# Placing VectorE operations that share GpSimd's port as they become due, and moving the last head-pair products into the last score banks

## Chip, cores and metric

One core of one Trainium2 chip. The metric is the device time of one execution in microseconds; lower is better. "Span" is the time from the first to the last instruction in a profiled execution, about 2 us less than the time.

## The reference

Two independent attention layers read different inputs, and their outputs stand side by side. S = 2048, D = 512, 32 heads of 16.

```python
# A: multi-query attention, one key/value head for 32 query heads
q = (x @ wq) -> heads;  k = x @ wk;  v = x @ wv
p = softmax(q k^T * 16**-0.5);  a = concat_heads(p v) @ wo
# B: linear attention with a learned feature map
phi = concat(softmax(u @ w_phi), softmax(-(u @ w_phi)))   # for u = q and u = k
b = concat_heads((phi_q @ (phi_k^T v)) / (phi_q @ sum(phi_k) + 1e-6)) @ wo
return concatenate([a, b], axis=-1)                        # [1, 2048, 1024]
```

Part A has 32 x 2048 x 2048 scores to exponentiate: 2048 tiles of 128 x 512. That is most of the time.

## The kernel before

The kernel contains a scheduler that runs when the program is built. It keeps a list of jobs with estimated durations, an estimated clock `te` per engine, and places one job after the other; the order that it finds is then fixed in the program. The chip never sees the estimates, only the order and the semaphore waits.

Jobs that matter here: `qk` (scores, PE), `ex` (exponentials of two tiles, ACT), `dq`/`dz`/`dS`/`dpv` (four tiles, a "quad", exponentiated by VectorE with a bit trick, shifted three times by GpSimd, then accumulated), `ac` (copy of a finished accumulation out of PSUM), `rc` and DMAs (its denominators inverted and broadcast), `on` (multiply by them), `qw` (three steps of divisions of part B), `kvfin`.

```python
LOCK = ("dS", "qw", "on", "kvfin")      # VectorE jobs that use the port shared with GpSimd
...
# run(): when can job j start on its engine?
t = max(r, self.pe_from(j, te) if eng == "pe" else te)     # r: ready, te: engine free
j.asked = t
if eng == "pool" or j.name[0] in self.LOCK:
    t = max(t, self.te_port)                               # and the port free
...
s, j = min(picks, key=lambda p: (p[0], p[1].asked))
if j.eng == "dve" and j.name[0] in self.LOCK:              # a GpSimd job about due? take that
    s, j = next((p for p in picks if p[1].eng == "pool" and p[1].asked <= s + self.NEAR
                 and self.te_port <= s + self.NEAR), (s, j))
...
# an accumulation leaves PSUM only after the multiply two blocks earlier: f_accS has two buffers
self.job(("ac", sc), "dve", 0.60, lambda: self.finish_sc(sc), prio=0,
         after=[("on", sc - 2)] if sc >= 2 else [], frees=[("acc", sc)])
...
def finish_sc3(self, sc):               # "on": both inputs in SBUF
    self.add("dve", lambda v: v.tensor_tensor(out=o, in0=accS[:, r, :], in1=R[:, r, :], op=ALU.mult), ...)
    if r: self.dmas(...)                # odd blocks: f_Ot into the other rows of f_On
...
def out_part(self, i):                  # last 512 queries: three head pairs of two row blocks, early
    for A in range(3): pe.matmul(ps[:, bank, :], lhsT=On[:, A, ...], rhs=self.wo_pad[:, A, :], ...)
def finish_last(self):
    for i in (0, 2, 1, 3): ...          # the other products, then the last block's denominators
```

## Time and profile before

| | before |
|---|---|
| time, median | 712.1 us |
| exponential instructions on ACT (two tiles each) | 710 |
| quads on VectorE | 157 |
| first exponential starts / last one ends | 8.8 / 697.2 us |
| from the last exponential to the end of the span | 12.7 us |

Read it as a sum: ACT works without a break between the two times in the fourth row, so what counts is how many exponentials it gets, what gaps it has, and how long the ends are. The lines are in the prediction.

### The profile page before, as it was taken

What the parts mean: (1) busy time and instruction counts of PE and PEld (TensorE: products, weight loads), DVE (VectorE), ACT (ScalarE), POOL (GpSimd) and SP (SyncE); (2) the same over time, 40 slices, a digit from 0 to 9 for tenths busy, and PEclk for the clock granted to TensorE, in tenths of its full rate; (3) what the DMA queues carried; (4) which work ended last, traced back from release to release, by engine and by line L of the source; (5) the groups of instructions that cost most, each with busy time, mean ns of one, the idle gap of its engine ahead of it and who ended that gap; (6) DMA issues with size and microseconds to landing.
All of it is one profiled execution on the core that took longest, in us unless ns stands there. A gap on an engine that the chain in (4) does not pass through costs nothing.

```text
span 709.9 us, 20307 instructions
## 1 busy us (share of the span) xinstructions
PE 682.6 (96%) x8606; PEld 207.0 (29%) x8609; DVE 602.6 (85%) x1009; ACT 689.3 (97%) x782; POOL 498.4 (70%) x507
## 2 busy tenths in 40 slices
PE   8999999999999999998999999999999999999986
PEld 3322222222222222222233223332323233323222
DVE  4797899999899898988879978798879888998772
ACT  5999999999999999999999999999999999999994
POOL 5378777777777877575858856778685856678781
PEclk9999999999999999999999999999999999999999
DMA  6712133110111201111101221101121012112012
GB/s 125 147 11 38 32 43 75 15 10 3 8 14 13 39 2 14 11 10 13 13 5 15 35 27 17 17 7 20 10 20 21 16 13 40 24 18 29 13 10 44
DMA packets 47898, 18.42 MB, mean 26 GB/s; under 512 B 38708, under 2 KB 45940, under 8 KB 47800
## 3 DMA queue, kind: packets, MB, share of 16 engines
q1 hardware_dynamic: 45544, 16.36, 18.1%
q8 instruction: 69, 1.13, 0.7%
q10 hardware_dynamic: 2256, 0.69, 0.4%
q14 instruction: 29, 0.24, 0.1%
HBM read 2.28 MB, written 4.19 MB: 9 GB/s over the span
## 4 chain that ended last, share of the span: by engine, by line
ACT 60%; PE 31%; DVE 4%; POOL 1%; DMA 1%; SPq 1%; issue 1%; POOLq 0%; DVEq 0%
ACT f_PT L1701 57%; PE f_ps L1646 11%; PE f_ps L1866 8%; PE f_ps L1748 4%; DVE f_Z L1806 2%; ACT f_Ek L2127 2%; PE f_ps L1955 1%; PE f_ps L2319 1%; POOL f_Z L1836 1%; PE f_ps L2225 1%; ACT f_ET L2231 1%; PE f_ps L1443 1%; PE f_ps L2275 1%; PE f_ps L2300 1%; PE f_ps L1628 1%
## 5 line engine op out<-in xcount | busy, mean ns | idle before, releaser
L1701 ACT ACTIVATE f_PT<-f_ps 128x1024 bf16<-128x1024 f32 x710 | 661.9, 1124 | 4.3 <-PE f_ps L1748 2.3
L1836 POOL INT64_ADD f_Z<-f_Z x471 | 489.0, 1038 | 192.3 <-DVE f_Z L1806 153.3
L1806 DVE TENSOR_SCALAR f_Z<-f_ps 128x512 int16<-128x512 f32 x628 | 418.2, 684 | 74.3 <-PE f_ps L1646 69.9
L1646 PE MATMUL f_ps<-f_QA,f_KR 32*128 32x512 bf16 x2048 | 284.9, 385 | 13.0 <-ACT f_PT L1701 9.4
L1866 PE MATMUL f_ps<-f_Z,f_VK 128*32 128x512 f16 x2512 | 216.8, 385 | 5.0 <-PE f_ps L1866 1.8
L1646 PEld LDWEIGHTS f_ps<-f_QA,f_KR 32*128 32x128 bf16 x2048 | 72.1, 91 | 272.4 <-ACT f_PT L1701 252.7
L1748 PE MATMUL f_ps<-f_PT,f_VA 128*32 128x512 bf16 x1420 | 133.0, 385 | 0.1
L1866 PEld LDWEIGHTS f_ps<-f_Z,f_VK 128*32 128x32 bf16 x2512 | 53.1, 94 | 95.2 <-issue 58.5
L1748 PEld LDWEIGHTS f_ps<-f_PT,f_VA 128*32 128x32 bf16 x1420 | 34.1, 94 | 50.6 <-issue 45.2
L1443 PE MATMUL f_ps<-f_ones,f_zero 128*128 128x512 bf16 (+6 forms) x109 | 21.7, 371 | 1.5 <-POOL f_zero L1462 1.3
L2286 DVE TENSOR_TENSOR f_Wk<-f_ps,f_wq 128x512 bf16<-128x512 f32 x32 | 21.7, 681 | 0.4 <-PE f_ps L2275 0.4
L2172 DVE TENSOR_TENSOR f_vS<-f_ps,f_rs 128x1024 bf16<-128x1024 f32 x16 | 21.2, 1322 | 0.0
L1449 DVE COPY f_accS<-f_ps 128x512 f32<-128x512 f32 x31 | 21.0, 677 | 0.0
L2162 PE MATMUL f_ps<-f_Bwv,f_BxT 128*32 128x512 bf16 x256 | 19.6, 383 | 0.3
L2225 PE MATMUL f_ps<-f_BxT,f_Wq 128*32 128x512 bf16 x256 | 19.6, 383 | 0.2
L1628 PE MATMUL f_ps<-f_AxT,f_wq 128*32 128x512 bf16 (+1 forms) x272 | 19.5, 371 | 0.3
L2319 PE MATMUL f_ps<-f_Bwo,f_oT 128*32 128x512 bf16 x256 | 19.6, 382 | 0.1
L2119 PE MATMUL f_ps<-f_Wk,f_BxT 128*32 128x512 bf16 x256 | 19.6, 383 | 0.0
L2231 ACT ACTIVATE f_ET<-f_ps 128x512 bf16<-128x512 f32 x32 | 19.6, 740 | 0.0
L2127 ACT ACTIVATE f_Ek<-f_ps 128x512 bf16<-128x512 f32 x32 | 19.4, 726 | 0.0
L2133 DVE TENSOR_REDUCE f_ssum<-f_Ek 128x64 f32<-128x1024 bf16 x16 | 19.3, 1206 | 0.0
L1933 DVE TENSOR_TENSOR f_On<-f_accS,f_denS 128x512 bf16<-128x512 f32 x16 | 11.2, 702 | 7.4 <-DMA f_denS<-f_denS 7.4
(96 smaller groups left out, 274.5 us busy)
## 6 DMA issues: line engine op xcount, KB each, us to landing
f_denS<-f_denS SPq DMA_DIRECT2D x124, 30.0 KB, 3.1
out_dram<-f_outB SPq DMA_DIRECT2D x16, 128.0 KB, 2.4
f_denC<-f_accS SPq DMA_DIRECT2D x124, 2.0 KB, 1.7
f_denS<-f_denC SPq DMA_DIRECT2D x124, 2.0 KB, 1.7
out_dram<-f_outA SPq DMA_DIRECT2D x15, 128.0 KB, 2.3
f_On<-f_Ot SPq DMA_DIRECT2D x60, 16.0 KB, 1.8
f_Bwv<-in_B_wqkv_dram SPq DMA_DIRECT2D x1, 512.0 KB, 4.7
f_Bwo<-in_B_wo_dram SPq DMA_DIRECT2D x1, 512.0 KB, 4.6
```

Source lines behind the costliest of these rows:

```text
L1443: mm = pe.matmul(ps[m * i:m * i + m, bank, 0:n].rearrange("p (a n) -> p a n", n=128), lhsT=zero[0:r, 0:m], rhs=rhs, start=start, stop=star ...
L1628: mm = pe.matmul(ps[32 * g:32 * g + 32, bank, a:a + n], lhsT=self.wq[:, dc, A * 128 + 32 * g:A * 128 + 32 * g + 32], rhs=xT[:, dc, qc * 51 ...
L1646: return pe.matmul(self.ps[:, bank, :], lhsT=self.KR[32 * g:32 * g + 32, sc % 2, kap * 128:(kap + 1) * 128], rhs=self.QA[32 * g:32 * g + 3 ...
L1701: self.add("act", lambda a: a.activation(out=PT[:, sl[0]:sl[0] + size, :], in_=ps[:, b0:b0 + size, :], func=ACT.Exp), reads=[("PS", b0 + i ...
L1748: mm = pe.matmul(ps[32 * g:32 * g + 32, bank, :], lhsT=VA[:, kap, :], rhs=PT[:, slots[g], :], start=start, stop=stop, tile_position=(0, 32 ...
L1806: self.add("dve", lambda v: v.tensor_scalar(out=o, in0=ps[:, bank, :], scalar1=self.Z1, scalar2=self.Z0, op0=ALU.mult, op1=ALU.add), reads ...
L1836: fn = lambda g: g.int64_add(out=b, in0=a, in1=256 * t * 0x1000100010001)
L1866: mm = pe.matmul(ps[32 * g:32 * g + 32, bank, :], lhsT=self.VK[:, t, kap, :], rhs=Zf[:, sl[g], :], start=start, stop=stop, tile_position=( ...
L2127: self.add("act", (lambda a, sg: (lambda e: e.activation(out=Ek[:, r, a, :, :], in_=ps[:, bank, :].rearrange("p (h f) -> p h f", h=32), fu ...
L2225: mm = pe.matmul(ps[32 * g:32 * g + 32, bank, :], lhsT=w[:, dc, G * 128 + 32 * g:G * 128 + 32 * g + 32], rhs=xT[:, dc, m * 512:(m + 1) * 5 ...
L2231: self.add("act", lambda e: e.activation(out=self.ET[:, sl, :], in_=self.ps[:, bank, :], func=ACT.Exp, scale=1.0 - 2.0 * a), reads=[("PS", ...
L2319: mm = pe.matmul(ps[32 * g:32 * g + 32, bank, :], lhsT=oT[:, r, C, 32 * g:32 * g + 32], rhs=self.Bwo[:, C, :], start=(C == 0), stop=(C == ...
```

## The change

The intent: a LOCK job that has waited long is no longer passed over for GpSimd work again and again; the spread of part B's work over time (`T_B`) is chosen anew for it; and at the end fewer products wait for the second-last block.

```diff
+    PATIENT = 6.0
-    T_B = (43.0, 620.0)
+    T_B = (40.0, 595.0)
@@ run()
-                        if eng == "pool" or j.name[0] in self.LOCK:
+                        if eng == "pool" or (j.name[0] in self.LOCK and t - r < self.PATIENT):
                             t = max(t, self.te_port)
...
-            if j.eng == "dve" and j.name[0] in self.LOCK:
+            if j.eng == "dve" and j.name[0] in self.LOCK and j.asked == s and s < self.te_port:
+                s = self.te_port
+            elif j.eng == "dve" and j.name[0] in self.LOCK:
                 s, j = next(...)
@@ jobs_a(), out_part(): two head pairs instead of three, after "on" 24..27 instead of 24..29
-            for A in range(3):
+            for A in range(2):
@@ new job "fa": three early terms of row blocks 0 and 2, in score banks 0 and 2, once the last scores are read
+            job(("fa", i), "pe", 0.65, ... self.out_first(2 * i) ..., after=[("on", 24 + a) for a in range(6)],
+                ok=lambda: self.last_qk is not None and ("ex", self.last_qk) in self.issued)
@@ finish_last()
-        for i in (0, 2, 1, 3):
-            terms = [(self.On[:, a, :], a) for a in range(3)] if i % 2 == 0 else []
+        for i in (1, 3, 0, 2):
+            terms = [(self.On[:, 2, :], 2)] if i % 2 else []
```

More of the change, by code (lines that the diff above doesn't have):

```diff
@@ L1241, in __init__ @@
         self.free = [4, 5, 6, 7]
-        self.part_no = None
+        self.part_no = self.last_qk = None
         self.rec = None
@@ L1555, in jobs_a @@
         for i in range(2):
-            job(("pp", i), "pe", 0.65, (lambda i: (lambda: self.out_part(i)))(i), mode="full", nb=1, prio=3.0,
-                after=[("on", 24 + a) for a in range(6)] + [("bk", 15), ("bv", 15)] + [("bq", 3, G) for G in range(4)])
+            job(("pp", i), "pe", 0.43, (lambda i: (lambda: self.out_part(i)))(i), mode="full", nb=1, prio=3.0,
+                after=[("on", 24 + a) for a in range(4)] + [("bk", 15), ("bv", 15)] + [("bq", 3, G) for G in range(4)])
             job(("ppc", i), "dve", 0.60, (lambda i: (lambda: self.out_part2(i)))(i), after=[("pp", i)], frees=[("pp", i)], prio=1)
+            job(("fa", i), "pe", 0.65, (lambda i: (lambda: self.out_first(2 * i)))(i), mode="full", prio=3.0, after=[("on", 24 + a) for a in range(6)],
+                ok=lambda: self.last_qk is not None and ("ex", self.last_qk) in self.issued)
         for sc in range(31):
@@ L1670, in next_qk @@
         if not us:
+            if self.last_qk is None:
+                self.last_qk = i - 1
             return
@@ L1973, in fn @@
             mm = None
-            for A in range(3):
-                mm = pe.matmul(ps[:, bank, :], lhsT=On[:, A, i * 256 + 128:i * 256 + 256], rhs=self.wo_pad[:, A, :], start=(A == 0), stop=(A == 2))
+            for A in range(2):
+                mm = pe.matmul(ps[:, bank, :], lhsT=On[:, A, i * 256 + 128:i * 256 + 256], rhs=self.wo_pad[:, A, :], start=(A == 0), stop=(A == 1))
             return mm
-        self.add("pe", fn, reads=[("On", A) for A in range(3)] + ["wo_pad", "wo_pad0"], writes=[("PS", bank)])
+        self.add("pe", fn, reads=[("On", A) for A in range(2)] + ["wo_pad", "wo_pad0"], writes=[("PS", bank)])
     def out_part2(self, i):
@@ L1981, in out_part2, with product, fn, out_first @@
         self.copy(self.part[:, i, :], self.ps[:, bank, :], [("PS", bank)], [("part", i)] + [("BxT", c) for c in range(4)])
+    def product(self, i, terms, start, stop):
+        ps = self.ps
+        def fn(pe):
+            mm = None
+            for n, (o, a) in enumerate(terms):
+                mm = pe.matmul(ps[:, i, :], lhsT=o[:, i * 128:i * 128 + 128], rhs=self.wo_pad[:, a, :], start=start and n == 0, stop=stop)
+            return mm
+        return fn
+    def out_first(self, i):
+        self.add("pe", self.product(i, [(self.On[:, a, :], a) for a in range(3)], True, False), reads=[("On", a) for a in range(3)] + ["wo_pad", "wo_pad0"], writes=[("PS", i)])
     def finish_last(self):
-        ps, lnd, part, oa, ACC = self.ps, self.lnd, self.part, self.outA, self.bank(("acc", 31))
+        ps, lnd, part, oa, ACC, product = self.ps, self.lnd, self.part, self.outA, self.bank(("acc", 31)), self.product
         H = 256
-        def product(i, terms, start, stop):
-            def fn(pe):
-                mm = None
-                for n, (o, a) in enumerate(terms):
-                    mm = pe.matmul(ps[:, i, :], lhsT=o[:, i * 128:i * 128 + 128], rhs=self.wo_pad[:, a, :], start=start and n == 0, stop=stop)
-                return mm
-            return fn
-        for i in (0, 2, 1, 3):
-            terms = [(self.On[:, a, :], a) for a in range(3)] if i % 2 == 0 else []
-            self.add("pe", product(i, terms + [(self.On[:, 3, :], 4)], True, False), reads=[("On", a) for a in range(4)] + ["wo_pad", "wo_pad0"], writes=[("PS", i)])
+        for i in (1, 3, 0, 2):
+            terms = [(self.On[:, 2, :], 2)] if i % 2 else []
+            kw = dict(writes=[("PS", i)]) if i % 2 else dict(accum=[("PS", i)])
+            self.add("pe", product(i, terms + [(self.On[:, 3, :], 4)], i % 2 == 1, False), reads=[("On", a) for a in range(2, 4)] + ["wo_pad", "wo_pad0"], **kw)
         for h in range(2):
```

## The prediction

> **What bounds the kernel now.** The first view is the page: busy times, then the costliest groups.
>
> ```profile
> PE 682.6 (96%) x8606; PEld 207.0 (29%) x8609; DVE 602.6 (85%) x1009; ACT 689.3 (97%) x782; POOL 498.4 (70%) x507
> L1701 ACT ACTIVATE f_PT<-f_ps 128x1024 bf16<-128x1024 f32 x710 | 661.9, 1124 | 4.3 <-PE f_ps L1748 2.3
> L1836 POOL INT64_ADD f_Z<-f_Z x471 | 489.0, 1038 | 192.3 <-DVE f_Z L1806 153.3
> L1806 DVE TENSOR_SCALAR f_Z<-f_ps 128x512 int16<-128x512 f32 x628 | 418.2, 684 | 74.3 <-PE f_ps L1646 69.9
> ```
>
> ACT computes softmax exponentials, two score tiles at a time (L1701). The table of windows (20 us each) shows ACT busy 20.00 of 20.00 in nearly all of them between 40 and 600 us, and its idle time before L1701 is 4.3 us in all. So ACT sets the pace: 661.9 / 710 = 0.932 us for two tiles. The time can shrink only if ACT gets fewer tiles, or if the few us before its first exponential (8.8 us) and after its last (697.2 us) shrink. There are 2048 tiles. VectorE does 628 of them with a bit trick (L1806) in groups of four ("quads", 157), and GpSimd makes three shifted copies of each quad (471 = 3 x 157). **The exchange rate:** one more quad on VectorE takes four tiles, or 2 x 0.932 = 1.86 us, from ACT, and costs VectorE 4 x 418.2/628 = 2.66 us. VectorE is 85% busy and idles 69.9 us waiting for scores to work on: there is room, and the question is why it is not used.
>
> The second view is the timeline of VectorE, GpSimd and the SyncE queue around 600 us. Each of the 32 accumulations ("blocks": one half of the head pairs and 512 queries) ends in a copy to f_accS, DMAs that invert and broadcast the denominator (L1892, L1903, L1909), and a multiply, L1933, called "on" in the plan.
>
> ```profile
> 593.34 3.35 SPq L1909 DMA_DIRECT2D f_denS<-f_denS  x4
> 607.07 3.39 SPq L1909 DMA_DIRECT2D f_denS<-f_denS  x4
> 621.07 1.04 POOL L1836 INT64_ADD f_Z<-f_Z  x1
> 621.62 1.03 DVE L1933 TENSOR_TENSOR f_Ot<-f_accS,f_denS 128x512 bf16<-128x512 f32 x1
> 622.57 0.68 DVE L1933 TENSOR_TENSOR f_On<-f_accS,f_denS 128x512 bf16<-128x512 f32 x1
> 623.17 0.68 DVE L1449 COPY f_accS<-f_ps 128x512 f32<-128x512 f32 x1
> ```
>
> The broadcast of block 25 was issued by 596.7 us and landed about 2.3 us later (3.1 us median from issue to landing, less its own 0.82 us of issue), so its multiply was due near 599; it ran at 621.62, and that of block 26, due near 613, right behind it. f_accS has two buffers, so block 27's copy (623.17) had to follow, and until then block 27's PSUM bank, one of four that the plan shares out, stayed held. I paired all 31 broadcasts with their multiplies: from the end of the last issue to the multiply 19.9 us on average (2.7 to 40.3), and in 13 of 29 blocks the f_accS copy came within 2 us of the multiply that it had to wait for. This is the plan's doing, not the chip's: operations in LOCK ("dS", "qw", "on", "kvfin") may only be placed where the plan's GpSimd is free, and a GpSimd job that is about due is preferred again and again.
>
> What a held bank costs shows in a table of windows: for twelve of those 13 copies, VectorE's busy time in the 10 us before the copy (first line) and in the 10 us after it (second).
>
> ```profile
> sum 120.00, DVE 100.23; mean DVE 8.35
> sum 120.00, DVE 110.03; mean DVE 9.17
> ```
>
> The third view is the end: the timeline of the SyncE queue and of VectorE, with the chain of waits, which runs through exactly these lines.
>
> ```profile
> 690.10 0.68 DVE L1933 TENSOR_TENSOR f_Ot<-f_accS,f_denS 128x512 bf16<-128x512 f32 x1
> 692.06 3.40 SPq L1909 DMA_DIRECT2D f_denS<-f_denS  x4
> 695.50 2.45 SPq L1939 DMA_DIRECT2D f_On<-f_Ot  x4
> 698.15 0.69 DVE L1933 TENSOR_TENSOR f_On<-f_accS,f_denS 128x512 bf16<-128x512 f32 x1 [7.37 <-DMA f_denS<-f_denS]
> 700.55 1.24 PE L1975 MATMUL f_ps<-f_wo_pad,f_On 128*128 128x512 bf16 x5 [0.56 <-DMA f_On<-f_Ot]
> 701.18 1.49 DVE L1449 COPY f_BxT<-f_ps 128x512 f32<-128x512 f32 x2 [2.34 <-PE f_ps L1975]
> 702.72 0.45 DVE L1999 STREAM_SHUFFLE f_ET<-f_ps 128x256 f32<-128x256 f32 x1
> ```
>
> The shuffle needs only the last accumulation, closed at 697.67 us. It starts at 702.72 because VectorE runs in order and stands behind two copies (L1449), which wait for products (L1975), which wait for the DMA of L1939.
>
> **What the Trainium skill says.** "SBUF — State Buffer", section "Who interferes with whom": a VectorE instruction with two SBUF inputs contends with a GpSimd instruction that reads SBUF, and the later one blocks until the other is done. The trace agrees: the GpSimd add above ends at 622.11, and the multiply that began at 621.62 ends 0.54 us after that and takes 1.03 us instead of 0.68. The longest multiply, 1.31 us, has the same cause. "VectorE: DVE Perf Modes", section "Why PSUM operands drop a tier": a PSUM operand rules out the two-port mode, so L1806 should not contend; its 628 instructions take 624 to 825 ns with GpSimd 70% busy. "Perfetto Trace Analysis", section "Identifying the Most-Contended Engine": matmul busy time is a poor measure. This trace bears it out in that the 96% of PE includes 21.7 us of filler on zeros (L1443), though most of PE's other work is real.
>
> **The change, part by part.**
>
> (a) Placement. A LOCK operation that was ready for 6 us (PATIENT) now competes at the time it became possible; if chosen, it starts when the plan's port is free. It removes the long starvation and leaves 6 us plus at most about one GpSimd add of 1.04 us. No instruction is added. The gain is VectorE time: raising those 13 stretches to the level after them gives 13 x (9.17 - 8.35) = 10.7 us. Part B's divisions ("qw") also finish sooner: the three steps took 20.8 us (447.3 to 468.2) and 16.1 us (591.7 to 607.8) in two of four blocks, 3.5 us in the others. 10.7 us would be 10.7 / 2.66 = 4 quads. Against it stands blocking on the port: some 25 multiplies and a few divisions are placed without regard to it; with GpSimd busy 70% and half an add of 1.04 us left on average, 35 x 0.7 x 0.52 = 13 us of VectorE at worst. I take half of that as falling into time in which VectorE waits for scores anyway, so 6.5 us or 2.4 quads lost. Net: 1.6 quads.
>
> (b) T_B. Part B's work is spread over 40 to 595 us instead of 43 to 620 (its last output copy was at 666.7). By itself this only moves VectorE load forward. But it is a retuned pair of numbers, chosen for this plan: I allow 1 quad for it, a guess. (a) and (b) together: 2.6 quads, 2.6 x 1.86 = 4.8 us, and ACT's total falls by the same.
>
> (c) The end. The early products take two head pairs instead of three (4 matmuls instead of 6), so they and their copies no longer wait for the DMA of L1939 and can run before the end. Products in banks 0 and 2 are split into three early terms (out_first) and one late. The matmuls number 20 before and after. The shuffle can start after the last multiply of L1933, 698.15 + 0.69 = 698.84 us, and what it feeds is done by 701.4 (the same steps took 702.72 to 705.28). PE then sets the end: if L1939 lands at the same 700.25, twelve products follow at 0.2125 us (sixteen took 700.55 to 703.95), to 703.1, four last ones to 703.95, and the last VectorE addition ends near 705.0 instead of 706.67: 1.7 us gained. If block 29's multiply comes early enough for L1939 to go ahead of the broadcast (L1909), the multiply at 698.84 limits: six products, the factors at 701.4, four last products, the addition to 703.0: 3.7 us gained. I take 2.4.
>
> Sum: 712.1 - 4.8 - 2.4 = 704.9.
>
> **The rivals.** (1) The port takes it back: starvation turns into blocked multiplies, each 1.0 to 1.3 us instead of 0.68, and the number of exponentials stays 710. For it: three multiplies show just this block. Against it: VectorE has 69.9 us of idle time to hide it in. Then only the end is won: 709.7. (2) Banks were the real limit: the multiplies on time free a bank for longer than the stretches I counted, VectorE reaches the 93 to 94% of its best windows (100 to 180 us: 18.2 to 19.6 of 20) everywhere. In the window of 660 us (20 to 680) it is at 579.5, 88%; solving 0.93 x (658 - 1.86 q) = 579.5 + 2.66 q gives 7.3 quads and about 696. Against it: the 10 us after a copy reach only 9.17 because delayed work is piled up there. (3) Another PE wait: out_first stands in PE's order and waits for L1939; if the plan lets it in before the last accumulation is finished, accumulation stalls behind a DMA; worth up to 3 us, so the end gains nothing: 707.
>
> **Range and chances.** The number of exponentials is decided by a greedy plan that answers chaotically to small changes: I give it 0 to 5 quads, 0 to 9.3 us, and the end 1 to 4 us. That spans 699 to 711; with rivals 2 and 3 at the edges I take 698 to 710. Faster by over 2% needs under 697.9, thus six quads and a good end: 0.11. Slower by over 2% needs some seven quads lost: 0.01.
>
> **What would show it.** L1701 some 5 fewer than 710 (x704 to x706), L1806 some 10 more than 628 (x640 or so), L1836 in step. The multiplies at most about 10 us after their broadcast, with more durations over 0.9 us than the three before. The f_accS copies evenly spaced near 21 us. The copies L1449 into f_BxT before the last exponential, the shuffle right behind the last multiply, and the time from the last exponential to the end near 10.3 us instead of 12.7. I am wrong if L1701 stays at 710 or grows (the placement is worth nothing), if it falls below 699 (rival 2), or if ACT has idle stretches of more than 5 us before its last exponential.

## The result

The change takes 706.12 us (705.97 to 706.59, 4 runs) against 712.06 us. The ratio is 0.9916, interval 0.9899 to 0.9933. (Ratios are the mean time of one kernel's runs over that of the other's of the same rounds, so not quite the ratio of the medians.) That is 5.9 us less: within 2%, inside the range, 1.2 us above the predicted 704.9.

The page of the kernel after, busy times and costliest groups, in the columns of those shown of before:

```profile
PE 678.6 (96%) x8614; PEld 205.4 (29%) x8614; DVE 609.7 (87%) x1017; ACT 686.6 (97%) x778; POOL 513.9 (73%) x513
...
L1705 ACT ACTIVATE f_PT<-f_ps 128x1024 bf16<-128x1024 f32 x706 | 658.1, 1107 | 4.4 <-PE f_ps L1648 3.3
L1840 POOL INT64_ADD f_Z<-f_Z x477 | 504.5, 1058 | 174.7 <-DVE f_Z L1810 135.4
L1810 DVE TENSOR_SCALAR f_Z<-f_ps 128x512 int16<-128x512 f32 x636 | 420.4, 682 | 55.9 <-PE f_ps L1648 51.6
```

(Lines have moved: L1701, L1806, L1836 and L1933 of before are L1705, L1810, L1840 and L1937.) VectorE took two more quads (636 tiles, 159 quads), so ACT runs 706 exponentials. VectorE waits 51.6 us for scores instead of 69.9. GpSimd's adds have become longer: 1058 ns on average instead of 1038.

The starvation is gone. From the end of a broadcast's issue to the multiply it takes 10.2 us on average instead of 19.9, at most 16.0 instead of 40.3. Before, 13 of 29 f_accS copies came within 2 us of the multiply that they had to wait for; now none does, and the copies are 16.5 to 25.8 us apart (10.2 to 33.5 before).

The end, in the timeline of the kernel after (start, duration, engine, line, output from input, count, and in brackets the idle time before it with what ended it):

```profile
688.69 3.43 SPq L1913 DMA_DIRECT2D f_denS<-f_denS  x4
...
692.16 2.45 SPq L1943 DMA_DIRECT2D f_On<-f_Ot  x4
...
694.81 0.69 DVE L1937 TENSOR_TENSOR f_On<-f_accS,f_denS 128x512 bf16<-128x512 f32 x1 [6.76 <-DMA f_denS<-f_denS]
...
695.61 0.44 DVE L2010 STREAM_SHUFFLE f_ET<-f_ps 128x256 f32<-128x256 f32 x1
...
696.87 2.77 PE L1994 MATMUL f_ps<-f_wo_pad,f_On 128*128 128x512 bf16 x12 [1.32 <-DMA f_On<-f_Ot]
...
699.47 1.03 PE L1994 MATMUL f_ps<-f_wo_pad,f_Ot 128*128 128x512 bf16 x4
```

The shuffle follows the last multiply at once. PE sets the end: its twelve products wait for the DMA of L1943, which still stands behind the broadcast (L1913).

**The sum.** I took the start and duration of every ACT instruction from the traces. An exponential follows the one before it after 0.917 us (median); "gaps" below is what the exponentials after the first took beyond 0.92 us each, summed.

| part of the span | before | after | difference |
|---|---|---|---|
| until the first exponential | 8.8 | 9.1 | +0.3 |
| exponentials x 0.92 us | 710 | 706 | -3.7 |
| gaps | 3.8 | 5.0 | +1.3 |
| other work of ACT between them (the rest) | 31.4 | 31.5 | 0.0 |
| after the last exponential | 12.7 | 9.4 | -3.3 |
| span | 709.9 | 704.5 | -5.4 |

(The row of exponentials gives counts, and the difference in us; rows are rounded.) Two thirds of what the quads were worth arrived, 2.4 of 3.7 us, and the end gave more (3.3 us). The questions for the experiments: which part did it, are the held banks really the cause, what made the new gaps, and why only two quads.

### The profile page after: what moved, and what is told of

It reads as the page before. It is cut to its first block, busy times and chain, and to the rows that moved or that the text cites. A ratio compares the mean times of both kernels' runs of the same rounds, so it can differ in the third digit from the quotient of the medians.

```text
span 704.5 us, 20334 instructions
## 1 busy us (share of the span) xinstructions
PE 678.6 (96%) x8614; PEld 205.4 (29%) x8614; DVE 609.7 (87%) x1017; ACT 686.6 (97%) x778; POOL 513.9 (73%) x513
## 4 chain that ended last, share of the span: by engine, by line
ACT 45%; PE 43%; DVE 8%; DMA 1%; SPq 1%; issue 1%; POOL 0%; DVEq 0%; POOLq 0%
ACT f_PT L1705 43%; PE f_ps L1648 15%; PE f_ps L1870 12%; PE f_ps L1752 6%; DVE f_Z L1810 4%; PE f_ps L1959 1%; PE f_ps L2330 1%; PE f_ps L2173 1%; PE f_ps L2130 1%; ACT f_ET L2242 1%; PE f_ps L1630 1%; PE f_ps L2236 1%; ACT f_Ek L2138 1%; PE f_ps L1443 1%; DVE f_vS L2183 1%
## 5 line engine op out<-in xcount | busy, mean ns | idle before, releaser
L1705 ACT ACTIVATE f_PT<-f_ps 128x1024 bf16<-128x1024 f32 x706 | 658.1, 1107 | 4.4 <-PE f_ps L1648 3.3
L1840 POOL INT64_ADD f_Z<-f_Z x477 | 504.5, 1058 | 174.7 <-DVE f_Z L1810 135.4
L1810 DVE TENSOR_SCALAR f_Z<-f_ps 128x512 int16<-128x512 f32 x636 | 420.4, 682 | 55.9 <-PE f_ps L1648 51.6
L1870 PE MATMUL f_ps<-f_Z,f_VK 128*32 128x512 f16 x2544 | 224.0, 386 | 5.7 <-PE f_ps L1870 3.1
L1870 PEld LDWEIGHTS f_ps<-f_Z,f_VK 128*32 128x32 bf16 x2544 | 54.1, 94 | 101.8 <-issue 69.1
L2297 DVE TENSOR_TENSOR f_Wk<-f_ps,f_wq 128x512 bf16<-128x512 f32 x32 | 21.7, 683 | 1.7 <-PE f_ps L2286 1.4
L1937 DVE TENSOR_TENSOR f_On<-f_accS,f_denS 128x512 bf16<-128x512 f32 x16 | 13.0, 813 | 6.8 <-DMA f_denS<-f_denS 6.8
L1443 PE MATMUL f_ps<-f_ones,f_zero 128*32 128x256 bf16 (+4 forms) x90 | 16.1, 367 | 1.3 <-POOL f_zero L1462 1.3
```

The lines of the kernel that those rows point to most:

```text
L1705: self.add("act", lambda a: a.activation(out=PT[:, sl[0]:sl[0] + size, :], in_=ps[:, b0:b0 + size, :], func=ACT.Exp), reads=[("PS", b0 + i ...
L1810: self.add("dve", lambda v: v.tensor_scalar(out=o, in0=ps[:, bank, :], scalar1=self.Z1, scalar2=self.Z0, op0=ALU.mult, op1=ALU.add), reads ...
L1840: fn = lambda g: g.int64_add(out=b, in0=a, in1=256 * t * 0x1000100010001)
L1870: mm = pe.matmul(ps[32 * g:32 * g + 32, bank, :], lhsT=self.VK[:, t, kap, :], rhs=Zf[:, sl[g], :], start=start, stop=stop, tile_position=( ...
```

## The experiments

All in one table; "tail" is from the last exponential to the end of the span, and times are medians with the ratio to the kernel before.

| run | what it is | exponentials | gaps | last exp. ends | tail | time | ratio [interval] |
|---|---|---|---|---|---|---|---|
| before | | 710 | 3.8 | 697.2 | 12.7 | 712.1 | |
| after | (a) + (b) + (c) | 706 | 5.0 | 695.1 | 9.4 | 706.1 | 0.9916 [0.9899, 0.9933] |
| end_only | (c) | 710 | 3.2 | 696.7 | 10.8 | 709.2 | 0.9955 [0.9938, 0.9972] |
| place_only | (a) | 706 | 4.9 | 695.1 | 10.4 | 706.7 | 0.9914 [0.9898, 0.9931] |
| place_end | (a) + (c) | 706 | 3.6 | 693.6 | 10.8 | 705.9 | 0.9904 [0.9888, 0.9921] |
| end_tb | (b) + (c) | 714 | 11.9 | 708.8 | 13.6 | 724.4 | 1.0173 [1.0156, 1.0190] |
| place_mul | (a), multiplies alone | 708 | 6.0 | 698.3 | 10.7 | 710.4 | 0.9969 [0.9953, 0.9986] |
| place_div | (a), divisions alone | 710 | 3.1 | 696.3 | 24.0 | 722.3 | 1.0149 [1.0132, 1.0166] |
| ring3 | before, third buffer | 704 | 7.8 | 695.9 | 30.7 | 728.0 | 1.0223 [1.0205, 1.0240] |
| no_lock | after, LOCK emptied | 702 | 11.7 | 697.8 | 9.2 | 708.9 | 0.9970 [0.9931, 1.0009] |
| no_port | after, multiplies off the port | 706 | 3.1 | 692.9 | 9.3 | 704.1 | 0.9886 [0.9870, 0.9903] |
| mul_on_gpsimd | after, multiplies on GpSimd | 702 | 367 | 1053.5 | 14.0 | 1072.1 | 1.506 [1.503, 1.509] |
| patient4 | after, patience 4, old T_B | 704 | 4.1 | 692.2 | 9.9 | 703.8 | 0.9880 [0.9863, 0.9896] |
| patient4b | patient4, T_B to 615 | 704 | 8.3 | 696.5 | 9.9 | 707.5 | 0.9932 [0.9918, 0.9945] |

### Which part: end_only, place_only, place_end, end_tb

**end_only**: the change with `PATIENT = 1e9` and the old `T_B`.

> Only part (c), the new end; placement and T_B as before. The built program has 710 exponentials, as before. My theory (the end is worth what PE and the last DMA leave, part of it): the last exponential ends as before near 697.2 us, and the time from there to the end falls from 12.7 to about 10.5 us, so 709.5 to 710.5 us in all. Rival 'the end is the whole gain': 706 to 707 us. Rival 'the early terms block PE': last exponential later than 698 us, time 711 or more.

709.16 us, 0.3 us below the expected range. The same 710 exponentials, a tail shorter by 1.9 us, and gaps shorter by 0.6 us.

**place_only**: the kernel before with the two conditions in run() and `PATIENT = 6.0` alone.

> Only part (a): PATIENT of 6 us in the plan of before; T_B and the end as before. The built program has 706 exponentials instead of 710. My theory (held banks cost quads, each worth 1.86 us): no f_accS copy waits for its multiply any more, waits of multiplies near 10 us, time 707.5 to 709.5 (2 quads, 3.7 us, less about 1 us of new waits). Rival 'the port takes it back on the chip': ACT gets idle time in place of the four exponentials, 711 to 713.

706.67 us, 0.8 us better than the expected range. The placement alone brings nearly all of the whole change, including 2.3 us of the tail, which I had put down to part (c): the multiply of block 29, no longer starved, comes earlier, and so does its DMA.

**place_end**: the change with `T_B = (43.0, 620.0)`.

> Parts (a) and (c) with T_B as before: the change less its retuned numbers. 706 exponentials, as with the whole change. My theory: T_B adds nearly nothing on the chip, so 705.5 to 707.5 us. Rival 'T_B is worth a quad or the plan's own 2.8 us': 708 to 709.5.

705.85 us, so the retuned T_B adds nothing: 0.9904 without it, 0.9916 with it, intervals overlapping. Part (c) on top of (a) is not resolved either (0.9914 and 0.9904). The profiles say why. First the timelines of the SyncE queue and of VectorE in place_only, then those in place_end:

```profile
690.08 2.45 SPq L1939 DMA_DIRECT2D f_On<-f_Ot  x4
...
692.51 0.69 DVE L1933 TENSOR_TENSOR f_On<-f_accS,f_denS 128x512 bf16<-128x512 f32 x1 [4.40 <-DMA f_denS<-f_denS]
```

```profile
682.12 3.12 SPq L1943 DMA_DIRECT2D f_On<-f_Ot  x4
...
689.67 4.00 SPq L1913 DMA_DIRECT2D f_denS<-f_denS  x4
...
695.83 0.69 DVE L1937 TENSOR_TENSOR f_On<-f_accS,f_denS 128x512 bf16<-128x512 f32 x1 [9.22 <-DMA f_denS<-f_denS]
```

In place_only the last multiply is done before the last exponential ends (695.1), and PE has what the DMA of block 29 brings at 695.2. In place_end the DMA goes ahead of the broadcast, as I had hoped for, but that puts the broadcast back, and the last multiply now comes 2.2 us after the last exponential. What one DMA gains in the queue the other loses.

**end_tb**: the change with `PATIENT = 1e9`.

> Parts (b) and (c) without (a): the new T_B and the new end with the old placement. The built program has 714 exponentials, two quads FEWER on VectorE than before. My theory: T_B was chosen for the new placement and harms the old one, 713 to 717 us. Rival 'T_B helps by itself': under 709.

724.37 us, slower still than I expected, in the direction of my theory. T_B by itself is no gain: with the old placement it costs two quads (714 exponentials) and 8.7 us of gaps against end_only.

### Which operations, and is it the held banks: place_mul, place_div, ring3

**place_mul** and **place_div**: place_only with the two new conditions for one name only.

```diff
-(j.name[0] in self.LOCK and t - r < self.PATIENT)
+(j.name[0] in self.LOCK and not (j.name[0] == "on" and t - r >= self.PATIENT))    # "qw" in place_div
-if j.eng == "dve" and j.name[0] in self.LOCK and j.asked == s and s < self.te_port:
+if j.eng == "dve" and j.name[0] == "on" and j.asked == s and s < self.te_port:    # "qw" in place_div
```

> Part (a) for the multiplies alone; divisions and kvfin stay starved; T_B and the end as before. The built program has 708 exponentials. If held banks are the main thing: about half of the quads and the earlier last DMA, 708 to 710. If the divisions are the main thing: 711 or more.

> Part (a) for the divisions alone; the multiplies stay starved; T_B and the end as before. The built program has 710 exponentials, as before. If held banks are the main thing: nothing gained, and in the plan the last multiplies come very late, so 712 to 722. If the divisions are the main thing: 709 or less.

710.39 us, just above its expected range, and 722.29 us, just above its own. The multiplies alone give one quad and the shorter tail, and lose part of that to gaps (6.0 us). The divisions alone give nothing and leave the end worse, with a tail of 24 us, because the last multiplies are starved: block 29's broadcast was issued by 678.5 us, the DMA after its multiply at 690.6, block 30's DMAs from 693.1 on, and the last multiply ran at 710.2. So the multiplies are what has to be placed. In these three orders the two together give one quad more than the multiplies alone; the rebuilt plans below show that this is not so in general.

**ring3**: the kernel before with three buffers for f_accS, f_denS and f_denC.

```diff
-    NZ = 14
+    NZ = 13
...
-after=[("on", sc - 2)] if sc >= 2 else []
+after=[("on", sc - 3)] if sc >= 3 else []
...
```

> The kernel before with a third buffer for f_accS, f_denS and f_denC, so that a late multiply holds no PSUM bank; the starvation itself stays. To make room NZ is 13 instead of 14, which gives the kernel before an identical plan. The built program has 704 exponentials. My theory (held banks are what the starvation costs): VectorE gets 3 quads more with the old placement, the last exponential ends near 692 us; but part B still ends late (starved divisions), so the end of the kernel may be longer; 705 to 711 us. Rival 'the held banks cost nothing, other things in the new placement do': last exponential at 696 us or later.

The count moved as the theory says: VectorE gets three quads more (704 exponentials). The time did not: 728.04 us. The group of exponentials on the page of ring3, then a line of its waits:

```profile
L1701 ACT ACTIVATE f_PT<-f_ps 128x1024 bf16<-128x1024 f32 x704 | 656.6, 1121 | 7.6 <-PE f_ps L1646 6.2
```

```profile
ACT f_ET L2003 <- DVE f_ET L1999: 23.8, 1, 23.8
```

After the last exponential ACT waits 23.8 us for the end's work (6.0 us before): outputs of part B are still being made after 700 us. The expected range for the time was missed for that reason, and the last exponential at 695.9 us lies between what the theory (692) and its rival (696 or later) said, so the run is evidence by its count alone. Nor is it the clean test that it was meant to be. The third buffer did not free the banks: the multiplies were put off further, to 33.6 us after their broadcast on average (66.6 at most) instead of 19.9, and 10 of 28 f_accS copies still came within 2 us of the multiply that they had to wait for, now the one three blocks earlier. Two copies right behind two multiplies, from the timeline of VectorE:

```profile
679.07 0.68 DVE L1933 TENSOR_TENSOR f_On<-f_accS,f_denS 128x512 bf16<-128x512 f32 x1
...
680.27 1.28 DVE L1449 COPY f_accS<-f_ps 128x512 f32<-128x512 f32 x2
```

One count can also be luck of one order. So the plans were built again without running them: five kernels, each over the same 32 pairs of T_B (starts 37, 40, 43 and 46; ends 560 to 630 in steps of 10). "Held" is the plan's own time from the end of a block's last accumulating product to the start of its copy, summed over 31 blocks.

| plan | quads, mean of 32 | banks held, us |
|---|---|---|
| before | 156.0 | 151 |
| third buffer (ring3) | 157.9 | 111 |
| multiplies alone (place_mul) | 158.8 | 19 |
| divisions alone (place_div) | 156.5 | 150 |
| all of LOCK (place_only) | 158.4 | 19 |

Each mean is uncertain by about 0.4. So placing the multiplies makes the quads, 2.8 on average, and placing the divisions makes none that stands out of the uncertainty; that place_only got one quad more than place_mul is the luck of these orders. Quads rise as the held time falls, which fits the held banks as the way from the multiplies to the quads, but no run shows that way by itself: ring3 changes how late the multiplies come as well. Where the placement of the change is in force, the third buffer leaves the plan's counts and times exactly as they are: no copy waits there.

### What the port takes back: no_lock, no_port, mul_on_gpsimd

**no_lock**: the change with `LOCK = ("dS",)`.

> The change with multiplies, divisions and kvfin taken out of LOCK: the plan places them without regard to GpSimd and believes that they cost 0.60 us. The built program has 702 exponentials against 706. Rival 1 (the port takes it back): over half of the 31 multiplies take 0.9 us or more, VectorE loses 10 us or more to them, and the time is no better than the change, 706 to 709. If the port hardly matters: 702 to 703.

As rival 1 has it: 708.88 us (one of its runs took 713.7) with four exponentials fewer than the change. 21 of the 31 multiplies take over 0.75 us, 9.8 us more in all than 31 x 0.683, and ACT has 11.7 us of gaps. Counts that the plan wins by ignoring the port are lost on the chip.

**no_port**: the change with a wrong result; each multiply becomes an operation with one SBUF input and the same waits.

```diff
-v.tensor_tensor(out=o, in0=accS[:, r, :], in1=R[:, r, :], op=ALU.mult)
+v.tensor_reduce(out=o, in_=accS[:, r, :].unsqueeze(2), axis=AX.X, op=ALU.max)
```

> The change with every multiply replaced by a maximum over one element of f_accS, with the same waits, order and output shape: one SBUF input, so it cannot contend with GpSimd. The result is wrong on purpose (the denominators are left out). Order and counts are those of the change, 706 exponentials. If the port takes part of the gain back on the chip, the multiplies all take about 0.68 us (5.6 us of excess gone), GpSimd's adds lose most of their 9.9 us of excess, the last exponential ends 1 to 4 us earlier than 695.1 us and the time is 702.5 to 705. If the blocking falls into time in which VectorE waits anyway, the time is that of the change, 705.5 to 706.5.

The multiplies of before, of the change and of no_port, from the view of one line (count, then shortest/median/longest in ns, first and last start):

```profile
L1933 DVE TENSOR_TENSOR f_On<-f_accS,f_denS x16: 677/683/990, 83.9 to 698.2; 128x512 bf16<-128x512 f32 x16
L1933 DVE TENSOR_TENSOR f_Ot<-f_accS,f_denS x15: 679/682/1309, 85.7 to 690.1; 128x512 bf16<-128x512 f32 x15
```

```profile
L1937 DVE TENSOR_TENSOR f_On<-f_accS,f_denS x16: 627/681/1543, 61.1 to 694.8; 128x512 bf16<-128x512 f32 x16
L1937 DVE TENSOR_TENSOR f_Ot<-f_accS,f_denS x15: 669/684/1464, 79.4 to 682.7; 128x512 bf16<-128x512 f32 x15
```

```profile
L1937 DVE TENSOR_REDUCE f_On<-f_accS x16: 625/674/686, 60.8 to 691.8; 128x512 bf16<-128x512 f32 x16
L1937 DVE TENSOR_REDUCE f_Ot<-f_accS x15: 629/674/677, 79.1 to 680.5; 128x512 bf16<-128x512 f32 x15
```

In the change 11 of 31 multiplies take over 0.75 us (3 before), 5.6 us of excess in all (1.3 before). In no_port none does, the excess of GpSimd's adds over 1037 ns falls from 9.9 to 1.5 us, and the gaps of ACT fall from 5.0 to 3.1 us, below those of the kernel before. The time falls to 704.05 us, ratio 0.9886 against 0.9916: 2.1 us. The order of the program is the same, so this is what the port costs the change on the chip: 2.1 of the 8.0 us that its order gains without the port, about a quarter. That "SBUF — State Buffer" of the Trainium skill ("Who interferes with whom") says a tensor_reduce never contends on trn2 agrees with these 31 instructions, 625 to 686 ns with GpSimd busy beside them.

**mul_on_gpsimd**: the change with the multiplies as GpSimd jobs of 1.2 us.

```diff
-job(("on", sc), "dve", 0.60, ...)
+job(("on", sc), "pool", 1.2, ...)
```

> The change with the 31 multiplies done by GpSimd, planned at 1.2 us each: VectorE loses 26.7 us of work and none of the multiplies can be blocked by the port or starved. The built program has 702 exponentials against 706. If VectorE time is what limits the quads: 2 quads, 3.7 us less, 702 to 704 us, with GpSimd some 45 us busier. Rival 'GpSimd becomes the bound': L1866/L1870-type products wait for GpSimd longer than the 20 us of before, and the time stays at 706 or above.

1072 us: neither theory foresaw this. The plan won four exponentials (702), and ACT stood still before its exponentials for 353 us. From the waits and the timeline of GpSimd:

```profile
ACT f_PT L1705 <- PE f_ps L1648: 330.8, 124, 12.9
...
POOL f_Z L1840 <- issue: 171.3, 29, 6.3
POOL f_On L1937 <- issue: 112.1, 16, 7.7
```

```profile
315.80 3.31 POOL L1840 INT64_ADD f_Z<-f_Z  x3 [0.17 <-DVE f_Z L1810]
325.97 1.25 POOL L1937 TENSOR_TENSOR f_On<-f_accS,f_denS 128x512 bf16<-128x512 f32 x1 [6.87 <-issue]
```

The multiply itself takes 1.25 us, as planned. But each change from the 64-bit add to the multiply costs some 7 us in which GpSimd waits for nothing that the profile shows, and each change back some 6 us (171.3 / 29): some 13 us per multiply, and 380.5 us in all (209.2 before 30 multiplies, 171.3 before 29 adds), about the 366 us lost. The program order is fixed, so PE, in order, waits for the shifted tiles (L1870 on L1840: 273.1 us), and ACT for PE. (The granted clock of PE was 0.81 in this run and 0.99 to 1.00 in the others; what that adds is not separated.)

The trace also shows what stands just before these gaps: instructions MODIFY_POOL_CONFIG, 120 at these two lines where the change has two. One line each from the views of the two lines:

```profile
L1937 POOLq MODIFY_POOL_CONFIG  x60: 10/11/13, 54.8 to 1050.8; - x60
...
L1840 POOLq MODIFY_POOL_CONFIG  x60: 1/1/12, 12.7 to 1028.7; - x60
```

The Trainium skill's "GPSIMD Engine Reference", section "Instruction dispatch", says that the first call to a freshly loaded kernel pays about 6 us with no instruction in the profile, counted from this instruction. The trace agrees: 6.6 to 7.7 us from it to the multiply. So these gaps are very likely such loads, one at each switch; the load itself is not in the profile.

### A better version? patient4, patient4b

**patient4**: the change with `PATIENT = 4.0` and `T_B = (43.0, 620.0)`. **patient4b**: the same with `T_B = (43.0, 615.0)`.

> A candidate for a better version: the change with a patience of 4 us and T_B as before. The built program has 704 exponentials, one quad more than the change. By the exchange rate 704 to 705.5 us. If the extra blocking and a later part B eat it: 706 to 709.

> The better candidate once more with another order: patience 4 us, T_B of 43 to 615 instead of 43 to 620. The built program has 704 exponentials too. If the number of exponentials is what counts, it is as good: 703 to 705 us. If 703.8 was the luck of one order: 705.5 to 709.

patient4 takes 703.82 us, 0.2 us below its expected range, correct and the fastest here, 0.9880 of the kernel before. patient4b has as many exponentials and takes 707.47. The waits of ACT, patient4 first:

```profile
ACT f_PT L1705 <- PE f_ps L1648: 2.4, 6, 0.7
...
ACT f_PT L1705 <- PE f_ps L1752: 0.2, 1, 0.2
```

```profile
ACT f_PT L1705 <- PE f_ps L1648: 4.1, 7, 1.1
...
ACT f_PT L1705 <- PE f_ps L1752: 2.1, 3, 1.0
```

The gaps, 8.3 against 4.1 us, are the whole difference. So 703.8 is in part the luck of one order: two programs with equal counts lie 3.7 us apart, as much as two quads. Nor does a shorter patience bring quads on average: built again over the same 32 pairs of T_B, the change has 157.5 quads on average with a patience of 4 us, 158.3 with 6 and 159.0 with 12. What about an order makes these gaps is not settled; blocked multiplies (15 against 11) can be only part of it.

## Why the prediction was right

The time (704.9 for 706.1) and the range were right, and so was the mechanism in its main steps: ACT sets the pace, the starved multiplies cost VectorE quads, and placing them brings quads. That the held PSUM banks are what costs them is likely, but not shown. The terms of the sum:

- **The exchange rate held.** Four exponentials fewer are 3.7 us by the median of 0.917 us.
- **Quads, 2.6 predicted, 2 measured.** The share of the placement was 1.6 and is 2: place_only has the same 706. The quad that I allowed for T_B, called a guess, was wrong: T_B adds none.
- **The 10.7 us of the held banks** were overstated, and the prediction had no control. The 16 other f_accS copies, which waited for no multiply, show a step too, from 8.58 to 9.01 us of VectorE work in the 10 us before and after:

```profile
sum 160.00, DVE 137.25; mean DVE 8.58
sum 160.00, DVE 144.18; mean DVE 9.01
```

  So 0.43 of the 0.82 us is there without a held bank; and the thirteenth waiting copy, left out of the windows, shows no step (9.62 and 9.64). With all 13 and less the control, some 4 us are left by this method: 13 x (0.75 - 0.43).
- **Blocking** came to 6.0 us in the trace: 4.3 us more in the multiplies and 1.7 us in two steps of kvfin (1.12 us instead of 0.28). That is half of the 13 us worked out; that it is close to the 6.5 us subtracted is luck, since those were what was left after a halving. With both terms mended the method gives hardly a quad (4 us, less 3 to 6 us), so that its 1.6 quads came near the 2 measured is luck too.
- **The step that failed:** the blocking was counted as lost VectorE time alone. It also reached ACT, as gaps, and cost 2.1 us of time by no_port. The sum of 4.8 us had no such term, and the last exponential came only 2.1 us earlier.
- **The divisions** hardly finished sooner, against what I had said: their three steps took 45.5 us over the four blocks before and 42.4 after.
- **The end, 2.4 predicted, 3.3 measured** in the span. PE set it, as in my first case, but the DMA that it waits for landed 1.7 us after the last exponential instead of 3.0. That is a gift of the placement: place_only has a tail of 10.4 without the new end. I had counted the parts as additive. In the tail (c) alone gains 1.9 us, (a) alone 2.3 and the change 3.3; in the time, 3.3 us by (c) alone, about 6 by (a) alone and 5.9 by the change, they overlap almost wholly.
- **The marks**: exponentials x706 (I said x704 to x706), f_accS copies evenly spaced, more long multiplies, shuffle right behind the last multiply: seen. Multiplies "at most about 10 us" after the broadcast: 10.2 is their mean, 16.0 the longest. The tail, 10.3 predicted, is 9.4.
- **The rivals.** Rival 1 (the port takes it back) is true for about a quarter, 2.1 of 8.0 us, not for all. Rival 2 (93% of VectorE everywhere) is refuted: 590.1 of 660 us between 20 and 680 us, 89%. (Its 7.3 quads were a slip: with its 658 us the equation gives 7.4, with the 660 us of the window 7.8.) Rival 3 was not seen in the change.

To the prediction's third citation: the 21.7 us of filler show work of no use in the 96% of PE, which is another reason to distrust busy time than the page's (pipelining); no run here tests that one.

What stays open: whether the held banks are the way from the multiplies to the quads, and what in an order makes gaps on ACT. The 18.3 us that VectorE waits less for scores are not 18.3 us of room: over the whole span its idle time fell by 12.5 us (span less busy time, 107.3 to 94.8), of which 5.4 us is the shorter span and 7.1 us more work.

## What to carry to other kernels

A scheduling rule that always yields ("place it when the other engine is free") starves its job when the other engine is busy 70% of the time, and the late result can hold a buffer that others need; give the wait a limit. Count what each part of a change does alone and together before crediting it: here one part did nearly all, a retuned number nothing, and another mattered only where the first was missing. Where a plan answers chaotically, average the counts of many plans, which needs no run. Check in the trace that a test which was meant to remove a cause has removed it. Where a build-time plan ignores contention, the counts that it improves can be paid back as gaps in the engine that sets the pace, so compare instruction counts and gaps separately.

## What the Trainium skill lacked or had wrong

- "GPSIMD Engine Reference" (section "Instruction dispatch") has the load of some 6 us for the first call to a freshly loaded kernel. It does not say that alternating a 64-bit add with an ordinary tensor_tensor brings a MODIFY_POOL_CONFIG and such a pause at every switch: 7 us before each of 30 multiplies (209.2 us in all) and 5.9 us before each of 29 adds after them.
- "SBUF — State Buffer" (section "Who interferes with whom") is right that the later instruction blocks. It has slowdowns of one engine at a time; no page says how large the effect is on both sides of a mixed stream. Here 11 of 31 multiplies of 0.68 us took up to 1.54 us, GpSimd's adds lost 9.9 us in all, and the core 2.1 us.
